# VectorE's share of the exponentials in a four-layer attention kernel: seven passes in place of eight, and four banks a unit in place of two

## The chip, the cores and the metric

The kernel runs on one core of a Trainium2 chip. The engines that matter here are TensorE (PE, matrix products into PSUM), ScalarE (ACT, the exponential), VectorE (DVE, elementwise work and the reading of PSUM), GpSimd (POOL, masks and some transfers) and SyncE (SP, transfers). They run side by side and wait for each other by semaphores; each works through its own instructions in their order. The metric is the time of one execution on the device in microseconds, lower is better. Before the change the median of three runs was 2258.31 us (2255.68 to 2261.54).

## The reference

Four layers are applied to one sequence of 2048 tokens with 640 features, in bf16. Layers 0 and 2 use windowed causal attention (a query sees its own and the 255 keys before it), layers 1 and 3 full attention over all 2048 keys without a mask. There are 32 heads of 20 features each.

```python
def block(x, wqkv, wo, mask):
    q, k, v = split(layernorm(x) @ wqkv)          # 32 heads, Dh = 20
    scores = einsum("bhqd,bhkd->bhqk", q, k) * Dh ** -0.5
    if mask: scores = where(mask, scores, -1e9)   # layers 0 and 2
    p = softmax(scores)
    return x + einsum("bhqk,bhkd->bhqd", p, v).reshape(B, S, D) @ wo

x = block(x, A_wqkv, A_wo, window)   # layer 0
x = block(x, B_wqkv, B_wo, None)     # layer 1
x = block(x, A_wqkv, A_wo, window)   # layer 2
x = block(x, B_wqkv, B_wo, None)     # layer 3
```

The full layers need 32 x 2048 x 2048 exponentials each, and these two layers are most of the work.

## The kernel before

**Units, banks and tiles.** A sequence of 2048 queries is four chunks of 512 (`C`), and the 32 heads are eight groups of four (`G`). A unit (class `Unit`, L672) is one layer, one chunk of queries and one group. In a full layer its work is 64 banks: 16 blocks of 128 keys times four heads, each a score matrix of 128 keys by 512 queries that fills one of the eight PSUM banks. One round of the main loop (a tick, from L1279) takes a tile of two to four banks: TensorE computes the scores (L1316), ScalarE takes the exponential of the whole tile out of PSUM into a bf16 tile `pt` (L1347), and two or three ticks later TensorE multiplies `pt` by the values into the output bank `op` (bank 7, L1380). Even ticks use PSUM banks 0 to 2, odd ticks 3 to 5 and, if nothing else has it, bank 6. A tile's banks can be written again only when its readers are done, two ticks later. The 21st value column is ones, so row 20 of the output holds the sum of exponentials; the division comes later (`t_tail`).

**What is interleaved.** Projections, layer norms, output projections and tails are generators (`Task`) that `pump` (L249) advances between the score and value products of a tick, by due time and credit. After the first phase they share one PSUM bank, number 6 (`take_m`, L264): TensorE fills it, VectorE evacuates it (`evac` L321, the residual sum L566, the scaling L1092), and only then it is filled again. `keep_clock` (L649) adds idle products on `masks` where a tick has too little TensorE work (L298, `ps<-masks,ident`); its aim per tick, `state["least"]`, is in proportion to the banks that ScalarE gets in that tick. Order on each engine is the order in which the code issues (`manual_schedule`); no scheduler moves it.

**VectorE's side work.** Not all banks go to ScalarE. A unit's tuple `aside` (L682) names banks (key block, head) whose exponential VectorE computes. In layer 1 these are two a unit in chunks 1 to 3 (24 units); in layer 3, chunks 1 to 3, they are four or six (23 units, 53 pairs). In layer 1 the side bank is the last bank of an ordinary tile: L1226 to L1233 place it when the tile count has reached three times the number already placed, so the tile has two banks for ScalarE and one for VectorE. In layer 3 the score goes to bank 6 (L912).

The generator `t_side` (L897) does two banks (a pair) at a time: two passes of 512 columns out of PSUM (L918), then six of 1024 columns in SBUF (L923 to L949), the last of which writes bf16 to an output slot. It takes the exponential by its bits: the score times log2(e), scaled by 2^23, goes to a whole number whose high bits are the exponent and whose low 23 bits are the fraction; the exponent bits and a fourth-degree polynomial of the fraction are multiplied. After every pass the generator yields that pass's cost (0.7 or 1.2); `side_step` (L956) spends it from a credit that grows each tick by 0.4 in layer 1 and by `SIDE_RATE` 1.1 in layer 3 (L1402). The three work tiles of layer 1 are slices of the early raw output (`raw_o`), with two output slots (`side_early`, L887); in layer 3 they are free `xnT` tiles with five slots. At the unit's end TensorE multiplies the finished pairs by their values (L1389), and the slots come free.

The order of the units (L730 to L746) puts layer 2's windowed units between those of layer 1: after groups 2 to 5 of each chunk come two of them, in which GpSimd's selects (L1419) and VectorE's mask products (L1429) run.

Of the kernel before, what the change touches and what calls it, by code (L numbers as in the profile page):

```python
# [9 lines left out]
BF16 = mybir.dt.bfloat16  # L10
F32 = mybir.dt.float32
I32 = mybir.dt.int32
ALU = mybir.AluOpType
ACT = mybir.ActivationFunctionType

# [5 lines left out]
NT = S // P  # L21
KD = D // P
G = 8
C = 512
NC = S // C
EPS = 1e-5
SCALE = DH ** -0.5
# [2 lines left out]

E23 = 2.0 ** 23
LOG2E = 1.4426950408889634
EA, EB, EC, ED = -0.10468731, 1.17604568, 0.83196789, 0.24582313
KA = 18
SIDE_RATE = 1.1
QA = 4

PARTS = {  # L40
# [6 lines left out]
def kernel(  # L47
# [58 lines left out]
    op = ps[:, 7, :]  # L106
# [565 lines left out]
    class Unit:  # L672
        def __init__(self, l, c, g, part=None):
            self.l, self.c, self.g, self.part = l, c, g, part
            self.windowed = l % 2 == 0
            self.aside = ()
            if self.windowed:
                sets = [(m, b0, subs, j) for m, b0, subs in window_banks(c) for j in range(4)]
            else:

                if c > 0 and (l, c, g) != (3, 1, 0):
                    self.aside = tuple((NT - 1, j) for j in ((2, 3) if l == 1 else range(4)))  # L682
                    if l == 3 and (c < 3 and g % 2 and (c, g) != (2, 7)):
                        self.aside += ((NT - 2, 0), (NT - 2, 1))
                    if l == 1 and False:
                        self.aside += ((NT - 1, 0), (NT - 1, 1))
                k0, k1 = key_blocks(l, part)
                sets = [
                    (None, 0, [(kc, 0, 4, 0)], j) for kc in range(k0, k1) for j in range(4)
                    if (kc, j) not in self.aside  # L690
                ]
            n = len(sets)
            self.banks = [
                (self, j, m, b0, subs, i < 4, i >= n - 4 + len(self.aside), i == n - 1)
                for i, (m, b0, subs, j) in enumerate(sets)
            ]
# [200 lines left out]
    def t_side():  # L897

        V = nc.vector
        while aside:  # L900
            u = aside[0]
            for pair in range(len(u.aside) // 2):
                while id(u) not in loaded or (u.l == 3 and not side["late"]):
                    yield None
                for i in range(2):
                    yield "bank"
                    xi, xm, xw = side["tiles"]
                    if u.l == 3:
                        mseq[0] += 1
                        mfree[6] = (state["tick"] + 2, mseq[0])  # L910
                        kc, j = u.aside[2 * pair + i]
                        nc.tensor.matmul(  # L912
                            ps[:, 6, :], lhsT=u.k(kc, j), rhs=u.q(j, 0, 4), start=True, stop=True
                        )
                        side["psum"] = ps[:, 6, :]
                    scored = side.setdefault("scored", {})
                    scored[id(u)] = scored.get(id(u), 0) + 1
                    V.tensor_scalar(  # L918
                        out=xi.bitcast(I32)[:, i * C : (i + 1) * C], in0=side["psum"],
                        scalar1=SCALE * LOG2E * E23, scalar2=-128.0 * E23, op0=ALU.mult, op1=ALU.max,  # L920
                    )
                    yield 0.7
                V.tensor_scalar(  # L923
                    out=xm.bitcast(I32), in0=xi.bitcast(I32), scalar1=0x7FFFFF, scalar2=0x3E800000,
                    op0=ALU.bitwise_and, op1=ALU.bitwise_or,
                )
                yield 0.7
                V.tensor_scalar(
                    out=xi.bitcast(I32), in0=xi.bitcast(I32), scalar1=0x7F800000,
                    scalar2=0x40000000, op0=ALU.bitwise_and, op1=ALU.bitwise_xor,  # L930
                )
                yield 0.7
                V.scalar_tensor_tensor(  # L933
                    out=xw, in0=xm, scalar=EA, in1=xm, op0=ALU.add, op1=ALU.mult
                )
                yield 1.2
                V.scalar_tensor_tensor(  # L937
                    out=xm, in0=xw, scalar=EB, in1=xm, op0=ALU.mult, op1=ALU.add
                )
                yield 1.2  # L940
                V.scalar_tensor_tensor(
                    out=xw, in0=xw, scalar=EC, in1=xm, op0=ALU.add, op1=ALU.mult
                )
                yield 1.2
                while not side["out"]:
# [1 line left out]
                pt = side["out"].popleft()  # L947
                po = pt.rearrange("p a b -> p (a b)")
                V.scalar_tensor_tensor(  # L949
                    out=po, in0=xw, scalar=ED, in1=xi, op0=ALU.add, op1=ALU.mult  # L950
                )
                side_out.setdefault(id(u), []).append(pt)
                yield 1.2
            aside.popleft()

    def side_step(bank):  # L956
# [246 lines left out]
    with tc.manual_schedule():  # L1203
# [12 lines left out]
        tiles = []  # L1216
# [4 lines left out]
        while n < last_layer:  # L1221
# [3 lines left out]
            extra = []  # L1225
            if (  # L1226
                len(at) < len(u.aside) and banks[n + 1][0] is u
                and len(tiles) >= 3 * len(at) + (at or [0])[0]
            ):
                kc, j = u.aside[len(at)]  # L1230
                extra = [(u, j, "side", 0, [(kc, 0, 4, 0)], False, False, False)]
# [47 lines left out]
        while ended is None or t < ended + 8:  # L1279
# [119 lines left out]
                    break  # L1399

            if n_b:
                side["credit"] = min(side["credit"] + ((SIDE_RATE if state["unit"] < index[3, NC - 1, 0, None] else 0.95) if side["late"] else 0.4), 1.2)  # L1402
                side_step(False)

            if t > 0 and masked is not None:
# [71 lines left out]
```

## Time and profile before

| what | value |
|---|---|
| median of three runs | 2258.31 us (2255.68 to 2261.54) |
| span of the profiled execution | 2253.6 us |
| ScalarE busy | 2159.6 us (96%) |
| TensorE busy | 1946.9 us (86%) |
| VectorE busy | 1253.3 us (56%) |
| GpSimd busy | 484.2 us (21%) |
| layer 1, chunks 1 to 3, side work on `raw_o` | 490 to 1302 us |
| layer 3, chunks 1 to 3, side work on `xnT` | 1598 to 2241 us |

The page gives the profiled execution's span, from its first to its last instruction, and no separate time for it; what lies around the span is in the runs' times alone. A row of a group is: line, engine, operation, output and inputs by the program's names, shapes, count, then busy time in us, mean ns of one, and the idle time before them with what ended it. A timeline row starts with the start and the duration in us; an answer on one tile has minimum, median and maximum duration in ns. Instructions of one engine overlap a little, so that the mean duration of one is longer than the distance between two.

### The profile page before, as it was taken

The numbers are of one execution on the slowest core, as the hardware profiler recorded it, in microseconds if no ns is written. First come the engines' busy times: TensorE is split into PE (matmuls) and PEld (weight loads), VectorE is DVE, ScalarE is ACT, GpSimd is POOL, SyncE is SP. The second block draws the span as 40 slices with busy tenths as digits, with TensorE's granted clock in tenths as the row PEclk, the third lists the DMA queues.
The fourth block names the chain that finished last, engine by engine and source line by source line (L and its number), as shares of the span: only waits on it lengthen the run. The fifth ranks groups of instructions, "written<-read, shape, count | busy, mean of one in ns | idle before, by whom it ended". The sixth has DMA issues, their size and how long they took to land.

```text
span 2253.6 us, 71223 instructions
## 1 busy us (share of the span) xinstructions
PE 1946.9 (86%) x30991; PEld 775.9 (34%) x30991; DVE 1253.3 (56%) x2150; ACT 2159.6 (96%) x1736; POOL 484.2 (21%) x950
## 2 busy tenths in 40 slices
PE   8999998988888888888888888898888888888887
PEld 4444443334333333333333443342322222222222
DVE  6656564436454555455553643242577667776666
ACT  7899899999999999999899999999999999999997
POOL 6674544201111124111331123312000000000000
PEclk9999999999999999999999999999999999999999
DMA  6233323422111233012320143113211111111100
GB/s 196 74 102 84 91 78 91 104 70 69 54 34 28 65 91 87 15 34 62 97 78 15 23 115 95 29 26 89 64 52 31 31 40 34 31 31 47 39 19 16
DMA packets 88408, 137.15 MB, mean 61 GB/s; under 512 B 20766, under 2 KB 63486, under 8 KB 88094
## 3 DMA queue, kind: packets, MB, share of 16 engines
q1 hardware_dynamic: 68878, 79.43, 13.2%
q0 software_dynamic: 19216, 53.17, 8.1%
q8 instruction: 242, 3.96, 0.8%
q14 instruction: 72, 0.59, 0.1%
HBM read 99.52 MB, written 27.79 MB: 56 GB/s over the span
## 4 chain that ended last, share of the span: by engine, by line
ACT 46%; PE 25%; issue 16%; DVE 10%; POOL 1%; DMA 1%; SPq 0%; ACTq 0%; DVEq 0%; POOLq 0%
ACT pt L1347 44%; PE ps L298 15%; PE ps L1316 6%; PE ps L1380 2%; ACT ka L1347 1%; DVE on L1092 1%; DVE st L321 1%; DVE x_sb L566 1%; PE ps L1088 1%; PE ps L435 1%; DVE pt L1429 1%; DVE va L321 1%; DVE vs L321 0%; DVE xnT L937 0%; DVE xnT L933 0%
## 5 line engine op out<-in xcount | busy, mean ns | idle before, releaser
L1347 ACT ACTIVATE pt<-ps 128x1536 bf16<-128x1536 f32 (+2 forms) x1634 | 2085.3, 1456 | 62.2 <-PE ps L1316 50.8
L298 PE MATMUL ps<-masks,ident 128*32 128x512 bf16 x6420 | 551.6, 388 | 114.3 <-ACT pt L1347 59.9
L1316 PE MATMUL ps<-qt,kt 32*128 32x512 bf16 x3990 | 545.3, 384 | 92.7 <-ACT pt L1347 84.9
L1380 PE MATMUL ps<-pt,vt 128*21 128x512 bf16 x3838 | 393.2, 382 | 0.1
L1316 PEld LDWEIGHTS <-kt 32*128 32x128 bf16 x3990 | 165.0, 91 | 551.4 <-issue 536.1
L1419 POOL TENSOR_SCALAR_AFFINE_SELECT pt<-pt 128x256 bf16<-128x256 bf16 (+2 forms) x505 | 216.3, 450 | 373.6 <-ACT pt L1347 333.1
L298 PEld LDWEIGHTS <-ident 128*32 128x32 bf16 x6420 | 165.9, 94 | 363.0 <-issue 350.0
L298 PE MATMUL ps<-xnT,wqk 128*32 128x512 bf16 x3320 | 220.6, 383 | 16.3 <-DVE st L321 8.1
L1429 DVE TENSOR_TENSOR pt<-pt,masks 128x512 bf16<-128x512 bf16 (+4 forms) x267 | 114.3, 440 | 177.7 <-ACT pt L1347 175.9
L321 DVE CAST st<-ps 128x512 bf16<-128x512 f32 x134 | 92.7, 692 | 197.9 <-PE ps L298 197.7
L298 PE MATMUL ps<-wop,on 128*32 128x320 bf16 x3712 | 156.9, 301 | 13.9 <-DVE x_sb L566 8.8
L918 DVE TENSOR_SCALAR xnT<-ps 128x512 int32<-128x512 f32 x106 | 73.3, 692 | 163.2 <-PE ps L912 162.3
L1316 PE MATMUL ps<-qa,ka 32*128 32x384 bf16 (+2 forms) x1408 | 118.2, 277 | 32.6 <-ACT pt L1347 29.7
L1380 PEld LDWEIGHTS <-vt 128*21 128x21 bf16 x3942 | 105.7, 91 | 115.3 <-issue 74.4
L298 PEld LDWEIGHTS <-on 128*32 128x32 bf16 x5760 | 116.6, 95 | 76.2 <-issue 54.1
L1092 DVE TENSOR_TENSOR on<-on,ps 128x512 bf16<-128x512 bf16 x128 | 86.4, 684 | 72.9 <-PE ps L1088 71.0
L298 PE MATMUL ps<-wv,xnT 128*32 128x320 bf16 x2560 | 112.4, 301 | 9.7 <-DVE on L1092 2.2
L566 DVE TENSOR_TENSOR x_sb<-x_sb,ps 128x320 bf16<-128x320 bf16 x120 | 58.2, 485 | 107.6 <-PE ps L298 107.5
L298 PEld LDWEIGHTS <-wqk 128*32 128x32 bf16 x3320 | 79.6, 96 | 110.9 <-issue 59.3
L864 DVE CAST on<-ps 128x512 bf16<-128x512 f32 x112 | 77.0, 687 | 44.4 <-PE ps L1380 29.7
L1316 PEld LDWEIGHTS <-ka 32*128 32x128 bf16 x1408 | 43.6, 92 | 116.7 <-issue 108.9
L402 POOL TENSOR_SCALAR rstd<-mv 128x4 f32<-128x4 f32 x15 | 3.7, 249 | 363.8 <-DVE mv L389 355.6
(101 smaller groups left out, 1655.3 us busy)
## 6 DMA issues: line engine op xcount, KB each, us to landing
vt<-v_d SPq DMA_DIRECT2D x48, 336.0 KB
kt<-k_d SPq DMA_DIRECT2D x192, 80.0 KB
wqk<-in_B_wqkv_dram POOLq DMA_DIRECT2D x80, 160.0 KB, 3.5
wqk<-in_A_wqkv_dram POOLq DMA_DIRECT2D x70, 160.0 KB, 3.6
k_d<-st POOLq DMA_DIRECT2D x75, 128.0 KB, 2.5
q_d<-st POOLq DMA_DIRECT2D x75, 128.0 KB, 2.5
qt<-q_d SPq DMA_DIRECT2D x384, 20.0 KB
v_d<-vs POOLq DMA_DIRECT2D x16, 336.0 KB, 3.6
```

Of the source, the lines that this page charges most:

```text
L298: nc.tensor.matmul(out_[r], lhsT=lhsT[:, r], rhs=rhs, start=start, stop=stop)
L321: nc.vector.tensor_copy(out=out_, in_=in_)
L435: nc.tensor.transpose(out=trp[32 * j : 32 * j + 32, dc, :], in_=xn[:, a : a + 32], identity=ident[:],)
L566: nc.vector.tensor_tensor(out=xv, in0=had, in1=yp, op=ALU.add)
L864: nc.vector.tensor_copy(out=oT, in_=op)
L918: V.tensor_scalar(out=xi.bitcast(I32)[:, i * C : (i + 1) * C], in0=side["psum"], scalar1=SCALE * LOG2E * E23, scalar2=-128.0 * E23, op0=AL ...
L1092: nc.vector.tensor_tensor(out=oT, in0=oT, in1=zb, op=ALU.mult)
L1316: nc.tensor.matmul(sp[:, i, col * P : (col + qn) * P], lhsT=u.k(kc, j), rhs=u.q(j, q0, qn), start=True, stop=True,)
L1347: nc.scalar.activation(out=pt[:, i:k, b0 * P :], in_=sp[:, i:k, b0 * P :], func=ACT.Exp, scale=SCALE,)
L1380: nc.tensor.matmul(op[32 * j : 32 * j + VW, q0 * P : (q0 + qn) * P], lhsT=u.v(kc, j), rhs=pg[:, i, col * P : (col + qn) * P], start=(first ...
L1419: nc.gpsimd.affine_select(out=v, in_=v, compare_op=ALU.is_gt if later else ALU.is_ge, fill=0.0, base=0, pattern=[[0, k - i], [-1 if later ...
L1429: nc.vector.tensor_tensor(out=pt_[:, i:k, cols], in0=pt_[:, i:k, cols], in1=mv_, op=ALU.mult)
```

## The change

Three things change. The exponential's eight passes become seven: the scaled score is now a 32-bit whole number whose upper halfword is the exponent and whose lower halfword is the fraction. One pass turns the lower halfwords (every second 16-bit word) into a float, already scaled and shifted for a cubic; one turns the upper halfwords into the bits of a bf16 power of two; two two-input passes compute the cubic, the second writing bf16 to the output slot; and a bf16 product multiplies the power in. In layer 1 each unit of chunks 1 to 3 gives four banks to VectorE, not two, at least 0, 3, 9 and 12 tiles after the first. And the credit per tick in layer 1 is 0.8, not 0.4.

```diff
-E23 = 2.0 ** 23
+FIX = 2.0 ** 16
-EA, EB, EC, ED = -0.10468731, 1.17604568, 0.83196789, 0.24582313
+E1, E0, EA, EB = 6.520200689873914e-06 * FIX, 0.7855486869812012, -1.118533968925476, 1.5344765186309814
 SIDE_RATE = 1.1
+SIDE_AT = (0, 3, 9, 12)
...
-                    self.aside = tuple((NT - 1, j) for j in ((2, 3) if l == 1 else range(4)))
+                    self.aside = tuple((NT - 1, j) for j in range(4))
...
-                        scalar1=SCALE * LOG2E * E23, scalar2=-128.0 * E23, op0=ALU.mult, op1=ALU.max,
+                        scalar1=SCALE * LOG2E * FIX, scalar2=-127.0 * FIX, op0=ALU.mult, op1=ALU.max,
...
                 V.tensor_scalar(
-                    out=xm.bitcast(I32), in0=xi.bitcast(I32), scalar1=0x7FFFFF, scalar2=0x3E800000,
-                    op0=ALU.bitwise_and, op1=ALU.bitwise_or,
+                    out=xm, in0=xi.bitcast(U16)[:, 0::2],
+                    scalar1=E1 / FIX, scalar2=E0, op0=ALU.mult, op1=ALU.add,
                 )
                 yield 0.7
+                power = xw.bitcast(I16)[:, 0 : 2 * C]
                 V.tensor_scalar(
-                    out=xi.bitcast(I32), in0=xi.bitcast(I32), scalar1=0x7F800000,
-                    scalar2=0x40000000, op0=ALU.bitwise_and, op1=ALU.bitwise_xor,
+                    out=power, in0=xi.bitcast(I16)[:, 1::2],
+                    scalar1=127.0, scalar2=128.0, op0=ALU.add, op1=ALU.mult,
                 )
                 yield 0.7
                 V.scalar_tensor_tensor(
-                    out=xw, in0=xm, scalar=EA, in1=xm, op0=ALU.add, op1=ALU.mult
-                )
-                yield 1.2
-                V.scalar_tensor_tensor(
-                    out=xm, in0=xw, scalar=EB, in1=xm, op0=ALU.mult, op1=ALU.add
-                )
-                yield 1.2
-                V.scalar_tensor_tensor(
-                    out=xw, in0=xw, scalar=EC, in1=xm, op0=ALU.add, op1=ALU.mult
+                    out=xi, in0=xm, scalar=EA, in1=xm, op0=ALU.add, op1=ALU.mult
                 )
                 yield 1.2
...
                 V.scalar_tensor_tensor(
-                    out=po, in0=xw, scalar=ED, in1=xi, op0=ALU.add, op1=ALU.mult
+                    out=po, in0=xi, scalar=EB, in1=xm, op0=ALU.add, op1=ALU.mult
                 )
+                yield 1.2
+                V.tensor_tensor(out=po, in0=po, in1=power.bitcast(BF16), op=ALU.mult)
                 side_out.setdefault(id(u), []).append(pt)
-                yield 1.2
+                yield 0.7
...
-                and len(tiles) >= 3 * len(at) + (at or [0])[0]
+                and len(tiles) >= SIDE_AT[len(at)] + (at or [0])[0]
...
-                side["credit"] = min(side["credit"] + ((SIDE_RATE if state["unit"] < index[3, NC - 1, 0, None] else 0.95) if side["late"] else 0.4), 1.2)
+                side["credit"] = min(side["credit"] + ((SIDE_RATE if state["unit"] < index[3, NC - 1, 0, None] else 0.95) if side["late"] else 0.8), 1.2)
```

The changed file is four lines shorter from here on, so that L1316, L1347, L1380 and L1389 of before are L1312, L1343, L1376 and L1385 after.

## The prediction

> **What bounds the kernel now.** I read the page first for the bound, then three windows of the span, then the waits inside the window that the change touches, then single rows for prices.
>
> ```profile
> span 2253.6 us, 71223 instructions
> PE 1946.9 (86%) x30991; PEld 775.9 (34%) x30991; DVE 1253.3 (56%) x2150; ACT 2159.6 (96%) x1736; POOL 484.2 (21%) x950
> ACT  7899899999999999999899999999999999999997
> ```
>
> ```profile
> 490.00:1302.00 812.00, 700.26 (x11308) 289.97 (x11308) 425.71 (x755) 790.94 (x621) 166.73 (x313) 1.00 0.21 55
> 1302.00:1598.00 296.00, 252.01 (x4114) 107.00 (x4117) 101.97 (x210) 287.22 (x212) 75.20 (x134) 1.00 0.27 72
> 1598.00:2254.00 656.00, 553.52 (x7222) 176.29 (x7214) 456.16 (x571) 639.88 (x467) 0.00 (x0) 0.99 0.12 35
> ```
>
> ScalarE is busy 96% of the span, so its exponentials are the clock of the kernel. The windows (columns: PE, PEld, DVE, ACT, POOL, granted clock, DMA share, GB/s) are the second layer's chunks 1 to 3 (490 to 1302 us), the stretch without side work, and the last layer's chunks 1 to 3. In the first, ScalarE is busy 97.4%, TensorE 86%, VectorE 52%: there is room on VectorE, and TensorE has 14%.
>
> ```profile
> L1347 ACT ACTIVATE pt<-ps 128x1536 bf16<-128x1536 f32 x1359 | 1871.7, 1554 | 54.5 <-PE ps L1316 43.8 <-POOL pt L1419 3.7 <-issue 2.8
> L1347 ACT ACTIVATE pt<-ps 128x1024 bf16<-128x1024 f32 x193 | 205.2, 1066 | 7.7 <-PE ps L1316 7.1
> ...
> L1429 DVE TENSOR_TENSOR pt<-pt,masks 128x512 bf16<-128x512 bf16 x98 | 45.1, 462 | 57.2 <-ACT pt L1347 56.3 <-POOL pt L1419 0.7
> ...
> L1429 DVE TENSOR_TENSOR pt<-pt,masks 128x768 bf16<-128x768 bf16 x58 | 34.1, 588 | 62.9 <-ACT pt L1347 62.7
> ```
>
> ```profile
> 1204.32 59.18 ACT L1347 ACTIVATE pt<-ps 128x1536 bf16<-128x1536 f32 x45
> ```
>
> Back-to-back exponentials overlap, so their mean durations (1554 and 1066 ns) overstate the step. Their ends in the trace lie 1343 ns apart for three banks, 917 ns for two and 1770 ns for four (medians). The unbroken run of 45 agrees: four of its tiles have two banks, and 41 x 1.343 + 4 x 0.917 = 58.7 us against 59.18. A bank taken off a saturated ScalarE is therefore worth 1343 - 917 = 426 ns, not 488.
>
> **The change, part by part.**
>
> *Banks.* Eight head groups in each of three chunks make 24 units; each gives VectorE four banks in place of two, so 48 banks move. In the built order, three-bank exponentials go from 1359 to 1318, two-bank ones from 193 to 241, four-bank ones from 26 to 21, one-bank ones from 15 to 14. The second layer's later chunks keep 608 ticks (rounds of the tile loop), because the moved bank still takes its place in the tile's PSUM. Ceiling: 48 x 0.426 = 20.4 us. In the last layer five four-bank tiles become three-bank ones: 21 x 1.770 + 449 x 1.343 against 26 x 1.770 + 442 x 1.343 + 0.49 is +0.1 us.
>
> The ceiling is not all collected. Summing what each exponential's end is late against those steps, this stretch loses 30.8 us in 608 ticks, in clusters (508 to 585, 790 to 870, 1062 to 1120, 1265 to 1302 us) where projections and layer norms are issued densely and TensorE, not ScalarE, sets the pace. I placed the 48 new two-bank tiles on the ticks of the old trace: near 29 there is next to no loss within four ticks (full 0.426 us: 12.4), near 9 a part (I take half: 1.9), near 10 over 0.5 us, where a shorter exponential only waits longer (0). Together 14.3 us; bounds 12.4 and 20.4.
>
> *TensorE.* The score and value matmuls are the same in number; 48 of the latter move from the running order (L1380) to the unit's end (L1389). The clock filler on masks goes from 6420 to 6248 strips, 43 groups of four at 0.39 us, about 17 us less TensorE work: it makes room for the shorter tiles and is on no path by itself. The granted clock is 1.00 here with 48 such tiles already; I cost it at nothing. POOL and SP keep their instruction counts and DMAs, and none is moved past another.
>
> *VectorE, cost of a pair of banks.*
>
> ```profile
> L918 DVE TENSOR_SCALAR raw_o<-ps x48: 675/692/693, 493.4 to 1285.0; 128x512 int32<-128x512 f32 x48
> L923 DVE TENSOR_SCALAR raw_o<-raw_o x24: 640/686/737, 497.5 to 1286.3; 128x1024 int32<-128x1024 int32 x24
> L928 DVE TENSOR_SCALAR raw_o<-raw_o x24: 693/694/853, 498.3 to 1287.0; 128x1024 int32<-128x1024 int32 x24
> L933 DVE SCALAR_TENSOR_TENSOR raw_o<-raw_o x24: 1172/1218/1220, 499.6 to 1289.5; 128x1024 f32<-128x1024 f32 x24
> ...
> L949 DVE SCALAR_TENSOR_TENSOR raw_o<-raw_o x24: 1215/1218/1226, 513.2 to 1302.0; 128x1024 bf16<-128x1024 f32 x24
> ```
>
> Before: 2 x 0.692 + 2 x 0.694 + 4 x 1.22 = 7.65 us. After: the two PSUM reads (1.38) stay, two 1.22 us passes stay, and a bf16 product of 1024 columns is new. The mask products give its price: 462 ns at 512 and 588 at 768 columns, so about 0.71. The two one-input passes now read every second halfword, a pattern no row shows. Lower bound: the same kind of pass on whole words, 0.694; upper: the 1.22 of a two-input pass on the same 1024 elements. I take 0.694, the nearer row (one input, both ends in SBUF). Sum 5.92 us (6.97 at the upper bound).
>
> The Trainium skill, "VectorE: DVE Perf Modes" (What auto-detection actually checks), lets one-input passes between SBUF tiles take two elements a cycle whatever the type, and four only for 16-bit data at step one. By it the halfword passes stay at about the whole-word price, and the second one, 16-bit at both ends, does not fall to a quarter.
>
> In 490 to 1302 us this makes 24 x 7.65 = 184 us into 48 x 5.92 = 284 us: VectorE goes from 426 to 526 us of about 800 (66%). In the last layer 53 pairs go from 405 to 314 us.
>
> *What VectorE's load costs.* It is off the path unless TensorE waits for it. One PSUM bank (6) serves all projection work here, and a side pass issued ahead of its evacuation holds it up:
>
> ```profile
> 788.08 0.64 DVE L923 TENSOR_SCALAR raw_o<-raw_o 128x1024 int32<-128x1024 int32 x1
> ...
> 788.75 0.69 DVE L928 TENSOR_SCALAR raw_o<-raw_o 128x1024 int32<-128x1024 int32 x1
> ...
> 789.36 0.48 DVE L566 TENSOR_TENSOR x_sb<-x_sb,ps 128x320 bf16<-128x320 bf16 x1
> ...
> 789.90 0.46 PE L298 MATMUL ps<-wop,on 128*32 128x320 bf16 x8 [0.87 <-DVE x_sb L566]
> ```
>
> The residual sum stands behind two side passes, and TensorE waits 0.87 us for it. Over the window TensorE waits 32.7 us for VectorE (95 times), of which 11.1 us (24 times) behind a side pass. With 1.54 times the side work that becomes 17; with the passes at twice the pace also standing closer (three in one tick instead of spread), up to twice that, 34: +6 to +23 us of TensorE waits, about half reaching ScalarE, as TensorE has 14% to spare: +3 to +11. A second bound: I tallied, tick by tick, the VectorE time placed in it less ScalarE's. VectorE is behind by 1.5 us or more in 13 of 608 ticks before and in 121 after. Before, ticks with such arrears lost 0.20 us each, those near 1 us 0.098, the rest 0.040; with the new counts the loss rises from 30.8 to 51, +20 us. That mixes cause and company: arrears come where TensorE is full anyway, and at four isolated places (around 788, 863, 1035 and 1064 us) arrears of 1.6 to 2.3 us cost nothing. I take +5, nearer the waits.
>
> *The side bank itself* sits in the exponential's PSUM and must be read before the next tile but one. Today the read ends on average 0.61 us before that tile's own exponential does, and TensorE's next but one can't start earlier, so another 0.6 us is free and TensorE's lead of one tile covers about one more. *The output slots*: two pairs now fill both, so a unit's first output waits for the previous unit's side products; these stand at least four ticks (5 us) earlier, so no wait.
>
> *POOL.* Selects beside a two-input mask product take 516 ns (256 columns) against 410 alone, so neighbours slow each other. But ticks with both a side pass and a select are 12 before and 12 after: nothing. The Trainium skill, "SBUF — State Buffer" (two separate sides), has VectorE passes with two SBUF inputs or in a two-port mode hold a port that GpSimd needs. Its rule would speak against doubling the side work; by it all 176 selects of the window, at the 0.11 us of that row, would cost POOL 19 us, against a forecast of none.
>
> *Last layer.* TensorE waits 16.4 us behind side passes there, ScalarE loses 7.8 us in all; with 23% less side time I take -1.5 us (bounds 0 and -4). The last pair's final pass stood at 2240.6 us, and now stands 35 ticks earlier; ScalarE's last tile still ends the stream, so nothing more.
>
> **Sum.** -14.3 + 5 - 1.5 + 0.1 = -10.7 us on the profiled span of 2253.6, so 2242.9; the median of the runs (2258.31) lies 4.7 above that span, the fastest 2.1. Applied to the median: 2247.6, given as 2247.
>
> **Rivals.**
> 1. *All of it is collected.* TensorE's lead absorbs everything: -20.4 - 2 = 2236. For it: the unbroken 45 tiles. Against: ten new tiles lie in clusters.
> 2. *TensorE takes the place of ScalarE.* It needs 86% of the present time; if each short tile is followed by a wait, only half of 14.3 remains, and +5 leaves -2: 2256, no change. For it: after today's 24 sequences of a two-bank tile and three full ones the loss is 65 ns higher than elsewhere; that is little.
> 3. *VectorE is late (slower than before).* If the halfword passes take 1.22 us each, side work is 335 us here and arrears of 1.5 us or more stand in 254 ticks: loss 69 against 30.8, +39, and 2258.3 - 14.3 + 39 = 2283. At 0.694 the same tally gives 2264. It decides from +14.3 us of ScalarE loss on, about 29 us more TensorE waits behind side passes: nearly fourfold, where work and pace together make threefold.
> 4. *The pass count buys nothing*: a pair stays at 7.65 us. Then 367 us here, worse than rival 3; no row supports it.
>
> **How the numbers follow.** A measurement of this kernel tells 0.3% (6.8 us) from no change. Forecast (2241 to 2251.5) 0.56, rival 1 0.14, rival 2 0.17, rivals 3 and 4 0.13. Faster is 0.70, same 0.17, slower 0.13. The range takes in rival 1 and 2 and leaves out most of 3: 2235 to 2263; the forecast's own is 2241 to 2252.
>
> **What the changed profile would show.** ScalarE's exponentials in that stretch ending 426 ns sooner at 48 more tiles; the halfword passes near 0.69 and the product near 0.71 us; VectorE about 526 us in some 800; TensorE's waits for L566's and L321's successors behind side passes at 17 to 34 us. Wrong, if those waits pass 40 us, if halfword passes take over 1 us, or if the granted clock falls below 0.99.

## The result, and the profile after

The changed kernel takes 2270.74 us (median of 8 runs, 2265.22 to 2279.18) against 2257.4 for the kernel before (8 runs, 2251.58 to 2264.54): a ratio of 1.0061 with a 95% interval of 1.0047 to 1.0076. It is 13.3 us slower, where the prediction had 10.7 us faster and a range up to 2263. Its profiled execution took 2268.53 us (2.2 below the median of its runs), with a span of 2266.8.

From the page of the changed kernel: the span, each engine's busy time, and ScalarE's row of slices.

```profile
span 2266.8 us, 71034 instructions
PE 1947.1 (86%) x30819; PEld 769.4 (34%) x30819; DVE 1249.3 (55%) x2241; ACT 2144.0 (95%) x1737; POOL 486.2 (21%) x950
...
ACT  7889899999999999999999899999999999999998
```

ScalarE has 15.6 us less work by this row, and the span is 13.2 us longer. VectorE is 4 us less busy than before in all. No engine has become the bound; ScalarE waits more. The windows say where (columns as in the prediction: PE, PEld, DVE, ACT, POOL, granted clock, DMA share, GB/s):

```profile
490.00:1320.00 830.00, 709.27 (x11305) 287.70 (x11305) 518.62 (x903) 790.92 (x632) 174.71 (x320) 0.99 0.20 57
1320.00:1615.00 295.00, 250.99 (x4129) 106.11 (x4128) 107.77 (x219) 286.33 (x212) 69.98 (x126) 1.00 0.23 64
1615.00:2266.00 651.00, 547.52 (x7035) 173.45 (x7031) 353.30 (x503) 624.82 (x457) 0.00 (x0) 0.99 0.12 34
```

These stretches are cut at round times. For a sharp comparison I cut by ticks instead, from the time stamps of the exponentials: the 608 ticks of layer 1's chunks 1 to 3, and layer 3 from its second chunk to its last exponential. "Work" is each exponential's step (1.343 us for three banks, 0.917 for two, 1.770 for four, as in the prediction), "loss" is the stretch less that work, that is, what ScalarE waited.

| us | layer 1, work | loss | time | layer 3, work | loss | time |
|---|---|---|---|---|---|---|
| before | 786.9 | 30.6 | 817.5 | 640.1 | 7.7 | 647.8 |
| after | 766.5 | 54.1 | 820.6 | 640.2 | 18.8 | 659.0 |
| difference | -20.4 | +23.5 | +3.1 | +0.1 | +11.1 | +11.2 |

The two stretches make up 14.3 us, the spans differ by 13.2. So the work fell by exactly the 20.4 us of the ceiling (48 x 0.426); layer 1 gave all of it back and 3.1 more, and layer 3, where the same exponentials run, lost 11 us on top. They are two separate faults.

ScalarE's groups by shape, after:

```profile
L1343 ACT ACTIVATE pt<-ps 128x1536 bf16<-128x1536 f32 x1318 | 1821.8, 1541 | 76.4 <-PE ps L1312 67.0 <-POOL pt L1415 2.7 <-issue 1.9
L1343 ACT ACTIVATE pt<-ps 128x1024 bf16<-128x1024 f32 x241 | 254.5, 1058 | 12.7 <-PE ps L1312 11.6
```

The counts are those of the built order (1318 and 241). The idle time ahead of them, waiting for score matrices (`ps` of L1312), is 78.6 us where it was 50.9: TensorE comes late.

**Layer 3: what TensorE waits for.** Waits of TensorE, 1600 to 2250 us (engine, what it was to write and its line, what it waited for: us, times, longest), after:

```profile
PE ps L301 <- ACT pt L1343: 49.9, 112, 0.9
PE ps L1312 <- ACT pt L1343: 12.0, 39, 0.6
PE ps L913 <- DMA kt<-k_d: 11.7, 7, 3.9
...
PE ps L301 <- DMA on<-on: 3.1, 1, 3.1
```

The kernel before has no wait for a DMA in this window. Now seven score products for VectorE (L913) wait 11.7 us for the keys of their unit, and an output projection 3.1 us for a tail's transfer. One of the seven in the timeline of the changed kernel (start, duration, engine, line; in brackets the idle time before it and what ended it; SPq is SP's queue):

```profile
2005.26 0.39 PE L1312 MATMUL ps<-qt,kt 32*128 32x512 bf16 x3 [0.37 <-ACT pt L1343]
...
2005.44 0.43 SPq L779 DMA_DIRECT2D vt<-v_d  x1
...
2008.87 0.27 SPq L793 DMA_DIRECT2D kt<-k_d  x1
...
2009.56 0.55 PE L913 MATMUL ps<-qt,kt 32*128 32x512 bf16 x1 [3.90 <-DMA kt<-k_d]
...
2010.43 1.07 PE L301 MATMUL ps<-masks,ident 128*32 128x512 bf16 x8
```

TensorE reaches the side product about when SP begins to issue the nine transfers of that unit; it stands 3.90 us on an instruction that nobody needs for many ticks, and the current unit's scores stand behind it. The filler strips after it take 1.07 us for eight, where they take 0.61 elsewhere. Windows of the same kernel show why:

```profile
2005.00:2010.00 5.00, 0.83 (x4) 0.18 (x3) 1.80 (x2) 2.90 (x3) 0.00 (x0) 0.96 0.51 145
2010.00:2014.00 4.00, 4.00 (x36) 0.90 (x39) 0.80 (x2) 1.70 (x2) 0.00 (x0) 0.62 0.08 24
```

TensorE was busy 0.83 of 5 us, and then its granted clock is 0.62 on average over 4 us (the last section has the pattern).

**Layer 1: what TensorE waits for.** Waits of TensorE for VectorE, before (490 to 1302 us):

```profile
PE ps L298 <- DVE st L321: 13.2, 43, 0.5
PE ps L298 <- DVE x_sb L566: 5.0, 12, 1.1
...
PE ps L298 <- DVE vs L321: 1.5, 4, 0.6
```

and after (490 to 1320 us):

```profile
PE ps L301 <- DVE st L324: 17.3, 43, 1.1
PE ps L301 <- DVE x_sb L569: 10.1, 22, 1.7
...
PE ps L301 <- DVE vs L324: 6.6, 10, 1.6
...
PE ps L301 <- DMA wqk<-in_B_wqkv_dram: 1.6, 1, 1.6
```

The same projections wait for the same evacuations of bank 6, longer and more often. In all, TensorE waits 59.0 us for VectorE in the stretch (33.2 before, by the same ticks), of which 36.5 us (65 times) stand behind a side pass, against 11.1 us (24 times). The changed kernel's longest:

```profile
510.70 0.69 DVE L924 TENSOR_SCALAR raw_o<-raw_o 128x1024 f32<-128x1024 uint16 x1
...
511.31 0.69 DVE L930 TENSOR_SCALAR raw_o<-raw_o 128x1024 int16<-128x1024 int16 x1
...
512.95 1.17 DVE L935 SCALAR_TENSOR_TENSOR raw_o<-raw_o 128x1024 f32<-128x1024 f32 x1
514.04 0.48 DVE L569 TENSOR_TENSOR x_sb<-x_sb,ps 128x320 bf16<-128x320 bf16 x1
...
514.57 0.46 PE L301 MATMUL ps<-wop,on 128*32 128x320 bf16 x8 [1.66 <-DVE x_sb L569]
```

Three passes and a layer norm's statistics stand ahead of the residual sum, and TensorE waits 1.66 us.

The last line of the list after is a third, small fault. At 1304.83 us a projection reaches weights whose transfer has not landed. TensorE waits 1.59 us, a stretch at half clock follows, and ScalarE loses 3.8 us between 1300 and 1315 us, where the kernel before loses 1.5. Of the other runs below, those with four banks a unit in most units wait here too (0.8 to 2.8 us); those with two banks have no wait for these weights. Why was not tried.

### The profile page after: what moved, and what is told of

It is laid out like the page before. It is cut to its first block, busy times and chain, and to the rows that moved or that the text cites. A ratio compares the mean times of both kernels' runs of the same rounds, so it can differ in the third digit from the quotient of the medians.

```text
span 2266.8 us, 71034 instructions
## 1 busy us (share of the span) xinstructions
PE 1947.1 (86%) x30819; PEld 769.4 (34%) x30819; DVE 1249.3 (55%) x2241; ACT 2144.0 (95%) x1737; POOL 486.2 (21%) x950
## 4 chain that ended last, share of the span: by engine, by line
ACT 44%; PE 26%; issue 15%; DVE 12%; POOL 2%; DMA 1%; SPq 0%; ACTq 0%; DVEq 0%; POOLq 0%
ACT pt L1343 42%; PE ps L301 16%; PE ps L1312 6%; PE ps L1376 2%; DVE on L1088 1%; DVE raw_o L935 1%; ACT ka L1343 1%; DVE x_sb L569 1%; DVE st L324 1%; DVE raw_o L919 1%; DVE raw_o L930 1%; DVE raw_o L943 1%; PE ps L438 1%; DVE vs L324 1%; DVE raw_o L924 1%
## 5 line engine op out<-in xcount | busy, mean ns | idle before, releaser
L1343 ACT ACTIVATE pt<-ps 128x1536 bf16<-128x1536 f32 (+2 forms) x1640 | 2077.9, 1431 | 89.0 <-PE ps L1312 78.6
L301 PE MATMUL ps<-masks,ident 128*32 128x512 bf16 x6248 | 540.4, 388 | 120.8 <-ACT pt L1343 56.4
L1312 PE MATMUL ps<-qt,kt 32*128 32x512 bf16 x3990 | 552.8, 385 | 80.9 <-ACT pt L1343 73.2
L1376 PE MATMUL ps<-pt,vt 128*21 128x512 bf16 x3810 | 387.5, 385 | 1.0 <-ACT pt L1343 1.0
L1312 PEld LDWEIGHTS <-kt 32*128 32x128 bf16 x3990 | 161.8, 91 | 543.4 <-issue 528.4
L1415 POOL TENSOR_SCALAR_AFFINE_SELECT pt<-pt 128x256 bf16<-128x256 bf16 (+2 forms) x505 | 215.7, 448 | 331.0 <-ACT pt L1343 320.4
L1312 PE MATMUL ps<-qa,ka 32*128 32x384 bf16 (+2 forms) x1408 | 116.4, 275 | 33.5 <-ACT pt L1343 30.5
L1376 PEld LDWEIGHTS <-vt 128*21 128x21 bf16 x3894 | 104.1, 92 | 116.7 <-issue 78.4
L919 DVE TENSOR_SCALAR raw_o<-ps 128x512 int32<-128x512 f32 x96 | 66.2, 689 | 55.3 <-PE ps L1312 52.7
L537 POOL DMA_DIRECT2D k_d<-st x75 | 43.9, 585 | 204.1 <-DVE st L324 192.4
```

The lines of the kernel that those rows point to most:

```text
L301: nc.tensor.matmul(out_[r], lhsT=lhsT[:, r], rhs=rhs, start=start, stop=stop)
L537: nc.gpsimd.dma_start(out=dst, in_=staging.pop())
L919: V.tensor_scalar(out=xi.bitcast(I32)[:, i * C : (i + 1) * C], in0=side["psum"], scalar1=SCALE * LOG2E * FIX, scalar2=-127.0 * FIX, op0=AL ...
L1312: nc.tensor.matmul(sp[:, i, col * P : (col + qn) * P], lhsT=u.k(kc, j), rhs=u.q(j, q0, qn), start=True, stop=True,)
L1343: nc.scalar.activation(out=pt[:, i:k, b0 * P :], in_=sp[:, i:k, b0 * P :], func=ACT.Exp, scale=SCALE,)
L1376: nc.tensor.matmul(op[32 * j : 32 * j + VW, q0 * P : (q0 + qn) * P], lhsT=u.v(kc, j), rhs=pg[:, i, col * P : (col + qn) * P], start=(first ...
```

## The experiments

Two questions follow: what made the waits in layer 3, and whether layer 1's loss is the amount of side work, its bunching, or TensorE's clock. One table for all runs; ratios are to the kernel before on the same chip, with 95% intervals, and as the runs were made on several chips, rows are compared by their ratios; losses and times by the ticks of the table above; "behind side" is what TensorE waited in layer 1 for VectorE with a side pass ahead; "halved" counts the stretches at half the granted clock.

| kernel | median us | ratio | layer 1 time, loss | behind side | halved | layer 3 time, loss | halved |
|---|---|---|---|---|---|---|---|
| before | 2257.4 | | 817.5, 30.6 | 11.1 | 1 | 647.8, 7.7 | 1 |
| after | 2270.74 | 1.0061 [1.0047, 1.0076] | 820.6, 54.1 | 36.5 | 6 | 659.0, 18.8 | 4 |
| e1_passes_alone | 2272.18 | 1.0062 [1.0047, 1.0078] | 815.8, 28.9 | 8.0 | 2 | 660.5, 20.3 | 5 |
| e2_hold | 2257.37 | 1.0006 [0.9995, 1.0018] | 821.8, 55.3 | 36.5 | 7 | 647.9, 7.7 | 3 |
| e3_late_pace | 2255.24 | 0.9992 [0.9982, 1.0001] | 819.8, 53.4 | 35.3 | 6 | 642.9, 2.8 | 0 |
| e4_light | 2257.41 | 0.9996 [0.9986, 1.0006] | 805.3, 38.9 | 17.2 | 2 | 660.1, 19.9 | 4 |
| e5_fill | 2255.34 | 0.9989 [0.9976, 1.0002] | 817.9, 51.4 | 32.6 | 3 | 643.7, 3.6 | 1 |
| e6_spread | 2250.02 | 0.9968 [0.9955, 0.9980] | 809.9, 43.5 | 23.4 | 3 | 644.9, 4.9 | 2 |
| e7_two_banks | 2251.35 | 0.9975 [0.9963, 0.9987] | 814.4, 27.5 | 8.0 | 1 | 645.4, 5.4 | 1 |
| e8_more_late | 2246.7 | 0.9953 [0.9940, 0.9967] | 810.6, 44.1 | 23.3 | 4 | 644.5, 18.2 | 4 |
| e9_before_fast_late | 2374.08 | 1.0519 [1.0503, 1.0536] | 817.6, 30.7 | | 1 | 766.0, 125.8 | 28 |
| e10_choice | 2242.49 | 0.9941 [0.9927, 0.9955] | 805.2, 34.5 | 20.2 | 1 | 645.4, 5.3 | 1 |

**e1_passes_alone**: the changed kernel with layer 1's banks and pace as before; only the seven passes remain.

```diff
-                    self.aside = tuple((NT - 1, j) for j in range(4))
+                    self.aside = tuple((NT - 1, j) for j in ((2, 3) if l == 1 else range(4)))
...
-  ... if side["late"] else 0.8), 1.2)
+  ... if side["late"] else 0.4), 1.2)
```

> The seven passes alone: two banks a unit in layer 1 and the credit 0.4 as before, the rest as changed. Theory A (two separate losses: in layer 1 TensorE waits behind the doubled side work; in layer 3 the cheaper pair lets the side work run ahead onto key transfers still under way): layer 3 stays as in the changed kernel, 656 us from its second chunk on, layer 1 is back at 815 to 817, total near 2257.4 + 9 - 1 = 2265, ratio 1.003 to 1.004. Rival B (everything comes from the four banks of layer 1, their shorter tiles and fewer idle products, and the clock that halves): no change from before or a little faster, 2252 to 2258, ratio 0.998 to 1.000.

Measured: 1.0062, as slow as the whole change, and above the 1.003 to 1.004 that was expected. Layer 1 is back at 815.8 us, as expected, and layer 3 has its full fault (660.5 us, expected 656). Waits of TensorE in this run, 1600 to 2250 us:

```profile
PE ps L913 <- DMA kt<-k_d: 11.5, 7, 3.7
...
PE ps L301 <- DMA on<-on: 3.4, 1, 3.4
```

The same seven waits: the cheaper passes alone bring them.

**e2_hold**: the changed kernel; in the last layer a unit's side work may begin eight ticks after its loads were issued, not at once.

```diff
+        loaded_at[id(u)] = state["tick"]
...
-                while id(u) not in loaded or (u.l == 3 and not side["late"]):
+                while id(u) not in loaded or (
+                    u.l == 3 and (not side["late"] or state["tick"] < loaded_at[id(u)] + 8)
+                ):
```

> The changed kernel, but in layer 3 the side work takes a unit's first bank at the earliest 8 ticks after that unit's transfers were issued. Theory A: TensorE's 11.7 us of waits for keys in the side score go, with the halved clock after them; layer 3 from its second chunk on at 647 to 650 us in place of 656, total 2261 to 2264, ratio 1.002 to 1.003. Rival C (layer 3 loses by its tails, whose transfers now stand behind a unit's loads in SyncE's queue): these keep their place here, so 2268 to 2271, ratio 1.005 to 1.006. Rival B: as C.

**e3_late_pace**: the changed kernel; the last layer's credit per tick falls to 0.73 of what it was. It was meant to fall like the price of a pair, but by the code's own units a pair goes from 7.6 to 5.9, not to 5.5, which is 0.78: a pair now takes about 7.4 ticks for 6.9 before the change, so the side work is a little slower than it was, too.

```diff
-SIDE_RATE = 1.1
+SIDE_RATE = 0.8
...
-  ... else 0.95) if side["late"] else 0.8), 1.2)
+  ... else 0.69) if side["late"] else 0.8), 1.2)
```

> The changed kernel, with layer 3's credit per tick cut from 1.1 to 0.8 (0.95 to 0.69 in the last chunk), in proportion to the pair's price (5.5 against 7.6 units of credit), so that a pair takes about as many ticks as before the change, and the tails' transfers stand where they did. Theory A and rival C: layer 3 back at 647 to 649 us, total 2260 to 2263, ratio 1.001 to 1.003. Rival B: 2268 to 2271, as the changed kernel.

Measured: both take the fault away, and both totals come out 4 to 5 us below what was expected. e2 brings layer 3 from 659.0 to 647.9 us, e3 to 642.9, with the passes unchanged (e2's profiled run lies 8.6 us above its median; some 7 us of that lie ahead of layer 1's stretch); e3 is 15.6 us below the changed kernel, by the ratios. e2 keeps the transfer's wait, e3 does not (no DMA line in its waits). e2, the same window:

```profile
PE ps L301 <- DMA on<-on: 2.8, 1, 2.8
```

The built order shows how they come. A unit's side work begins as soon as its transfers are issued, which is not when they have landed. Between a unit's loads and its first side product lay, for the 23 units in turn, 6, 26, 23, 28, 24, 29 ... 36, 37, 39 ticks before the change; after it 6, 18, 17, 16, 8, 13, 7, 14, 7, 13, 8, 14, 7, 13, 8, 7, 1, 2, 2, 2, 2, 1, 1. The pace had been set for eight passes; with seven the side work gains on the loads from unit to unit and catches them up at the seventeenth. Seven units stand at one or two ticks, and seven products wait. The eighth wait is the other half: side work that runs ahead takes bank 6 from the tails, so their transfers (L1101, `on` to `on`) are issued later, at one place in tick 1340 for 1334, and in four places behind a unit's nine loads on SP's queue. That place before:

```profile
1828.15 9.47 SPq L1105 DMA_DIRECT2D on<-on  x9
1841.95 0.36 SPq L778 DMA_DIRECT2D vt<-v_d  x1
```

and after, where the loads come first and the output projection then waits:

```profile
1844.54 0.27 SPq L793 DMA_DIRECT2D kt<-k_d  x1
...
1844.91 6.83 SPq L1101 DMA_DIRECT2D on<-on  x9
...
1853.06 0.46 PE L301 MATMUL ps<-wop,on 128*32 128x320 bf16 x4 [3.09 <-DMA on<-on]
```

ScalarE loses 16.3 us in four clusters around these waits (4.2 at 1856, 4.6 at 2013, 4.4 at 2153, 3.1 at 2183 us) of the 18.8 in all. That is more than the 14.8 that TensorE waits; a stretch at half clock goes with each of the four.

**e4_light**: the changed kernel with four banks a unit in layer 1, but a pair there costs four short passes (the two reads of PSUM, L924, and one copy to the output), so that VectorE carries less side work than before while ScalarE's tiles are those of the change. It leaves out the power of two and the cubic, so layer 1's result is not the exponential and the run counts as a time only.

```diff
+                if u.l == 3:
                     power = xw.bitcast(I16)[:, 0 : 2 * C]
...
+                else:
+                    V.tensor_scalar(out=po, in0=xm, scalar1=1.0, scalar2=0.0, op0=ALU.mult, op1=ALU.add)
```

> The changed kernel with layer 1's pair cut to two PSUM reads and two one-input passes (about 2.8 us in place of 5.9); the power of two, the cubic and its product are left out there, layer 3 is untouched. Banks, tiles and idle products of layer 1 are those of the changed kernel. Theory A: ScalarE's loss in layer 1 falls from 54 us to 30 or less, layer 1 from 820 to 797 or less, total 2245 to 2250, ratio 0.995 to 0.997. Rival B (shorter tiles with fewer idle products let the clock halve): loss stays above 45, total 2262 to 2271, ratio 1.002 to 1.006.

Measured: layer 1 takes 805.3 us, 15.3 less than in the changed kernel, with 17.2 us behind side passes in place of 36.5. The loss is 8.3 us above before, not 23.5: that is the most that the short tiles by themselves can cost, and the wait for weights (2.8 us here) is in it. It lies between the two expectations (30 or less, above 45): VectorE's load makes most of the rise, not all.

**e5_fill**: e3, and the least TensorE work per tick, up to which the filler on `masks` is issued, counts the banks given to VectorE too.

```diff
-                n_b = len(cur)
+                n_b = n_all = len(cur)
...
-                state["least"] = (1.76 if state["unit"] >= woven else 1.0) * n_b / 3
+                state["least"] = (1.76 if state["unit"] >= woven else 1.0) * n_all / 3
```

> As the run with layer 3's pace cut to 0.8, and the idle products' aim counts the side bank too, so that a two-bank tile gets the filler of a three-bank one. Theory A (the clock halves in layer 1 because TensorE waited for VectorE): the halvings in layer 1 stay near 6, its time at 818 or more, total 2255 to 2262, ratio 0.999 to 1.002. Rival B (it halves because the shorter tiles have too little filler): 2 or fewer halvings in layer 1, 8 to 12 us less there, total 2243 to 2248, ratio 0.993 to 0.996.

Measured: against e3, layer 1's halved stretches fall from 6 to 3, fewer than theory A and more than rival B expected; its time falls only from 819.8 to 817.9 us, not by rival B's 8 to 12, and the median does not move. So the clock is at most a small part of what costs layer 1 its gain; e4, with the change's own filler, has two halvings.

**e6_spread**: e3, and in layer 1 at most one side pass is issued in a tick (unless it is needed at once), so that the same passes stand apart.

```diff
+            if not side["late"] and not bank and not forced and side.get("tick") == state["tick"]:
+                return moved
...
             side["credit"] -= at
+            side["tick"] = state["tick"]
```

> As the run with layer 3's pace cut to 0.8, and in layer 1 at most one side pass a tick: same passes, banks, tiles and credit, but no two or three passes stand together. The ticks with VectorE 1.5 us or more in arrears fall from 121 to 36 (before the change 13). Theory A: the loss in layer 1 falls from 53 to 35 to 40 us, as with the light pair, its time from 820 to 802 to 807, total 2240 to 2246, ratio 0.992 to 0.995. Rival D (it is the amount of side work, not its standing together): 815 to 820 in layer 1, total 2250 to 2256, ratio 0.997 to 1.000.

Measured: the same tiles and the same passes, 9.9 us less in layer 1 than e3 (43.5 us lost for 53.4), 23.4 us behind side passes for 35.3; 2250.02 us, 0.9968. In the built order the ticks in which VectorE has 1.5 us or more of arrears fall from 121 to 36. Spreading the passes recovers about two thirds as much as taking most of them out (9.9 against e4's 15.3). The time lies between the two expectations (802 to 807, 815 to 820), so both the bunching and the amount count.

**e7_two_banks**: e1 with the late pace of e3, so the seven passes without the run ahead.

```diff
-                    self.aside = tuple((NT - 1, j) for j in range(4))
+                    self.aside = tuple((NT - 1, j) for j in ((2, 3) if l == 1 else range(4)))
...
-SIDE_RATE = 1.1
+SIDE_RATE = 0.8
...
+  ... else 0.69) if side["late"] else 0.4), 1.2)
```

> The seven passes with two banks a unit and credit 0.4 in layer 1, and layer 3's pace cut to 0.8. Theory A: layer 1 at 816, layer 3 from its second chunk on at 643, total 2250 to 2253, ratio 0.996 to 0.998: what the cheaper passes bring by themselves once layer 3 doesn't run ahead.

Measured: 2251.35 us, 0.9975 [0.9963, 0.9987], as expected: faster than before, and about 20 us below e1 by the ratios, from which it differs by the pace in the last layer alone. Against e7, e3 adds the four banks at twice the pace: 0.9992 against 0.9975, 3.8 us, with intervals that just overlap. So the part of the change meant to relieve ScalarE brings, as it was placed, no gain, and more likely a small loss.

**e8_more_late**: e6, with six banks for every unit of the last layer, a credit of 1.1 throughout that layer and e2's hold of eight ticks. What it computes is wrong for a cause left open, so it counts as a time only, and what it says is the weaker for it.

```diff
-                    if l == 3 and (c < 3 and g % 2 and (c, g) != (2, 7)):
+                    if l == 3 and (True):
```

> As the run with at most one side pass a tick in layer 1, but in layer 3 every unit from the second chunk on gives six banks to VectorE (69 pairs in place of 53), at the changed kernel's credit 1.1 and with the hold of 8 ticks after a unit's transfers. ScalarE's work in layer 3 falls by 14 us (four-bank tiles nearly vanish, 1626 ticks in place of 1628). Theory A: with VectorE at 0.9 of its time and the tails' transfers behind loads, waits take back a part: layer 3 at 632 to 645 in place of 643, total 2232 to 2248, ratio 0.989 to 0.996. If waits on transfers dominate as they did in the changed kernel: 650 or more, total 2250 to 2258.

Measured: 2246.7 us, inside the expected range. Layer 3 takes 644.5 us, as in e6 (644.9): ScalarE's work there falls by about 14 us, and its loss rises by 13. In this run more banks for VectorE buy nothing there either once side work comes as densely again.

**e9_before_fast_late**: the kernel before, its eight passes kept, with the last layer's credit raised so that side work runs ahead as after the change.

```diff
-SIDE_RATE = 1.1
+SIDE_RATE = 1.5
...
-  ... else 0.95) if side["late"] else 0.4), 1.2)
+  ... else 1.3) if side["late"] else 0.4), 2.4 if side["late"] else 1.2)
```

> The kernel before with its eight passes and two banks in layer 1, and only layer 3's credit raised: 1.5 a tick in place of 1.1 (1.3 in the last chunk), cap 2.4. The side work then reaches a unit's first bank 1 or 2 ticks after that unit's transfers were issued in the last seven units, as in the changed kernel (before: 6 ticks at the least, mostly 24 to 39). Theory A (running ahead onto transfers is the cause in layer 3, whatever the passes cost): seven waits for keys, 10 to 13 us, layer 3 at 656 to 662 in place of 648, total 2265 to 2272, ratio 1.003 to 1.006. If the new passes themselves matter: no change, 0.998 to 1.001.

Measured: 1.0519, far off what was expected. The waits for keys did come, but they are the smaller part. Waits of TensorE, 1600 to 2360 us, in this run:

```profile
PE ps L298 <- DVE rz L1053: 22.0, 11, 2.6
PE ps L298 <- DVE rT L1071: 21.3, 11, 2.6
PE ps L298 <- DVE on L1092: 17.9, 9, 2.8
...
PE ps L912 <- DMA kt<-k_d: 7.0, 6, 2.8
```

To let 1.22 us passes draw on the higher credit I had also raised its cap to 2.4, which lets several of them stand in a row ahead of the tails' VectorE steps. The run changed two things and so does not price the run ahead of eight passes. It does show bunching at its worst, beside the waits for transfers: ahead of each wait of 2 us and more for VectorE stand four side passes in a row (L928 to L941), the longest wait is 2.8 us, and 28 stretches at half clock go with them. One window of it:

```profile
2000.00:2100.00 100.00, 80.59 (x879) 20.92 (x875) 66.72 (x80) 82.18 (x60) 0.00 (x0) 0.83 0.10 30
```

**e10_choice**: e6, with two banks again for five of the 24 units: group 1 of each chunk and groups 6 and 7 of the last, which lie in the dense clusters.

```diff
+                    self.aside = tuple(
+                        (NT - 1, j)
+                        for j in ((2, 3) if l == 1 and (g == 1 or (c, g) in ((3, 6), (3, 7))) else range(4))
+                    )
```

> As the run with at most one side pass a tick in layer 1 and layer 3's pace at 0.8, but the units where four banks cost more than they gave there (group 1 of each chunk, groups 6 and 7 of chunk 3) give two again. Ticks with VectorE 1.5 us or more in arrears: 6, against 36. Summed by unit from the profiles of the runs with two and with four banks: 7.6 us less in layer 1, 802 to 806 in place of 810; total 2242 to 2248, ratio 0.993 to 0.996.

Measured, as expected: 2242.49 us, 0.9941 [0.9927, 0.9955], the fastest of all, about 13 us (0.6%) below the kernel before. 38 banks move for 48; ScalarE's work in layer 1 falls by 16.2 us (38 x 0.426), and only 3.9 us of it come back as loss. Windows of this run:

```profile
490.00:1302.00 812.00, 702.30 (x11267) 286.26 (x11267) 491.89 (x867) 789.17 (x630) 179.81 (x320) 1.00 0.21 58
1590.00:2236.00 646.00, 548.78 (x7106) 174.85 (x7106) 361.75 (x511) 631.13 (x461) 0.00 (x0) 0.99 0.12 34
```

The granted clock is back at 1.00 in the first; ScalarE is busy 789 of 812 us there, 776 of 812 in the changed kernel.

## Why the prediction was wrong, step by step

*Prices: right.* The changed kernel's passes on `raw_o` (times least/median/most in ns):

```profile
L919 DVE TENSOR_SCALAR raw_o<-ps x96: 672/692/693, 492.6 to 1298.5; 128x512 int32<-128x512 f32 x96
L924 DVE TENSOR_SCALAR raw_o<-raw_o x48: 643/693/741, 497.1 to 1299.7; 128x1024 f32<-128x1024 uint16 x48
L930 DVE TENSOR_SCALAR raw_o<-raw_o x48: 673/686/968, 497.7 to 1300.3; 128x1024 int16<-128x1024 int16 x48
L935 DVE SCALAR_TENSOR_TENSOR raw_o<-raw_o x48: 1172/1223/1226, 499.0 to 1301.7; 128x1024 f32<-128x1024 f32 x48
...
L947 DVE TENSOR_TENSOR raw_o<-raw_o x48: 636/683/693, 501.5 to 1304.3; 128x1024 bf16<-128x1024 bf16 x48
```

Every second halfword costs what whole words cost (0.686 to 0.693 us, forecast 0.694), the product 0.683 (0.71), a pair about 5.9 (5.92). The rule drawn from the Trainium skill, "VectorE: DVE Perf Modes" (What auto-detection actually checks), holds here: 16-bit data at a step of two stays at 0.686 us for 1024 elements. The condition of rival 3, passes of 1.22 us, did not occur, and rival 4 neither; the slower result came from elsewhere.

*Banks: right in size.* The step of 426 ns and the ceiling of 20.4 us are what ScalarE's work fell by, to the tenth.

*VectorE's load: the sign right, the size too small, and the first step that failed.* The waits behind side passes were put at 17 to 34 us and are 36.5. The rise of 25.4 us is just past the upper end of "+6 to +23", and "about half reaching ScalarE" was too little: the loss rose by 23.5, and with the 6.1 us that the bank term had already left uncollected taken off, 17.4 remain, 0.7 of each microsecond (0.6 if the wait for weights is taken off as well). TensorE's 14% to spare over the stretch did not absorb them. e6 shows a higher share: 11.9 us fewer such waits than in e3, 9.9 us less loss, 0.8. But the step that weighs most is "I take +5", near the lower end of both: it stands for some 10 us of waits, where 25 came. The text had a better number beside the one it took: the tally by tick, with a loss of 51 us (measured 54.1). It was discounted as mixing cause and company; e4 and e6, which change VectorE's load and spacing alone, show that most of it was cause. With +17.4 in place of +5 the two terms for layer 1 come to the measured +3.1, not -9.3.

*Last layer: the second step that failed, in sign.* "With 23% less side time I take -1.5 us (bounds 0 and -4)" stands against +11.2. The bounds held nothing of a wait that did not exist before. Two sentences carried the fault. One is "POOL and SP keep their instruction counts and DMAs, and none is moved past another": the tails' transfers were moved past the unit loads in four places. The other is "the last pair's final pass ... now stands 35 ticks earlier ... nothing more": that number is the run ahead itself, seen at its harmless end. Followed to its beginning, each unit's first side product stands earlier too, until the transfers it reads have not landed. With the pace held, the loss there does fall, by 2.3 to 4.9 us (e3, e5, e6, e7, e10), more than the -1.5 and up to a little past the bound of -4; as a pair is also spread over more ticks in these runs, that is not the price of the shorter passes alone.

*Clock: costed at nothing.* The mean stays at 0.99, yet six stretches at half clock stand in layer 1 for one. e5 halves their number and gains under 2 us, so in layer 1 they are a small price beside the waits; in layer 3 one lengthens what each long wait costs.

*What cost nothing, as said:* the read of the side bank and the output slots end none of the waits listed above, POOL ends 2.7 us of ScalarE's idle time (L1415) where it ended 3.7, and the stretch between the two layers takes 284 to 287 us in every run. The 176 selects were busy 79.4 us before and after: the 19 us that the prediction set against its "nothing" did not come.

The rivals: in layer 1 it went the way of rival 3, VectorE late, past its point of decision (+14.3 us of loss, measured +17.4 beside the 6.1), at the price of 0.694 for which that rival's tally gave 2264. The late keys, which no rival held, make the rest. By the ratios, the way from before to after goes: seven passes without the run ahead -5.6 us (e7), four banks at twice the pace +3.8 (e3 against e7), the faster pace with its run ahead +15.6 (after against e3). These are steps of one path, so that they add up proves nothing; e1 and e2 are the runs that test them from outside.

The prediction's own signs of being wrong were not passed: 36.5 us of waits for a limit of 40, 0.69 us for 1, a granted clock of 0.99 to two decimals for 0.99. None of them looked at the last layer, where half of the miss arose.

What stays open: what remains of layer 1's rise in loss (8.3 us in e4, 3.9 in e10) was not divided between the short tiles, the wait for weights and TensorE's own density there; and a run ahead with eight passes and an unchanged cap was not tried.

## What to carry to other kernels

When a step that is interleaved by credit gets cheaper, its pace changes too: follow where its first instruction stands against the transfers and buffers it needs, not only where its last one ends, and lower the credit with the price. Here TensorE, which works in its own order, stood up to 3.90 us for keys that were requested but not landed, though their product was needed only many ticks later. Moving work to an engine with room costs by how it is bunched ahead of a buffer that the bound engine's feeder shares: one pass a tick and leaving out the dense units made a 0.6% gain of what had been no gain at the held pace, with 38 banks moved in place of 48.

## What the runs showed of the hardware

TensorE's granted clock fell to half after gaps much shorter than I had thought of, and the profile shows a pattern. All thirteen stretches at half clock of the changed kernel start whole multiples of 3.413 us apart, and each lasts 3.41 us, once twice that (the last one is cut off by the end). So the clock here changes only at the bounds of a fixed row of intervals of 3.41 us. Ten of the stretches lie in the two parts compared above. For nine of them TensorE was busy at most 0.54 of the interval just before (0.03 to 0.54); for the one at 712.59 us it was busy 0.83, and its cause stays open. From 490 us to the last exponential one interval as empty was not followed by half clock (511.20 to 514.61 us, 0.51); all others that were not had 0.57 or more.

A wait by itself therefore decides little. In layer 1, five waits of 0.99 to 1.61 us have a stretch at half clock with them (near 535, 753, 1026, 1040 and 1306 us); seven others of 0.98 to 1.66 us, the longest of all among them (it ended at 514.57), have none. After the wait of 1.61 us that ended at 533.88 the clock stays full for more than a microsecond, until the next bound at 535.09:

```profile
534.50:535.00 0.50, 0.38 (x3) 0.09 (x1) 0.50 (x2) 0.24 (x1) 0.50 (x1) 1.00 0.72 139
...
535.50:536.00 0.50, 0.50 (x20) 0.40 (x16) 0.50 (x2) 0.29 (x1) 0.00 (x0) 0.50 0.92 185
```

At 1852.64 and 2146.18 us it falls while the wait is still on. Each of the four waits of 2.6 us and more in layer 3 has a stretch with it. Other runs also have stretches after busier intervals (0.61, 0.69 and 0.74 in e6), so a low share is not the whole rule.

The Trainium skill, "TensorE: Matmul & The Clock Gate" (Part 1: The HAM clock gate), has the half rate after an idle window of about 3.4 us. The length and the rate agree with these rows; a wholly idle window was not needed, as TensorE was busy for up to half of it and more.
